# Softmax maxima turned in mid-cycle and loaded right behind their store, in a kernel of attention and a Fourier layer

## The chip, the cores and the metric

One Trainium2 core runs the kernel. The metric is device time in microseconds (us), lower is better. The median of three runs of the kernel before is 1861.64 us (1859.5 to 1863.29).

## The reference

For a sequence of 2048 rows of width 640 it computes gated attention plus a Fourier layer, in float32:

```python
q, k, v = split(x @ wqkv)                     # 32 heads of 20
p = softmax(q @ k.T * 20 ** -0.5)             # per head, 2048 x 2048
a = (p @ v) @ wo
b = Re(DFT_seq(DFT_hidden(x2)))               # as products with given cosine and sine matrices
out = g * a + (1 - g) * b                     # g = sigmoid(sum(x * gate_w)) per row
```

## The kernel before, in words

**Units.** Two heads and half of the queries (1024) are one unit: 32 units, each of 32 steps. There are two passes over the scores of a unit. The maxima pass (`s_mm`, matmul L198, kind `m`) multiplies queries by keys, 128 x 512 scores at a time, and VectorE (DVE) takes the row maximum of each piece (L200). The exponential pass (`score`, matmul L951, kind `e`) multiplies keys by queries into the transposed scores, and ScalarE (ACT) takes the exponential (L953). Each step has two matmuls of each kind, one a head (`h`). The maxima pass runs `LEAD` = 41 steps ahead of the exponential pass.

**What ties the passes.** Queries and keys stand in `qst` and `kst` as 60 rows (three parts of 20). In the exponential pass the matmul has 62 rows: rows 60 and 61 of the queries hold the negative maximum, as a rounded value and a remainder, against ones in the keys. So the first L951 of a unit needs these rows. `max_chain` makes them: four small DVE operations, L228 to L232, of which the last (a transpose into `mtt`) is what "turned" means; then `store` (L235) writes `mtt` to the DRAM tensor `m_scr`, and `rows` (L239) loads two rows for each head from it into the query tile, with two DMAs. Since DRAM lies between, the SP queue waits at L239 until the store has landed.

**The order of work** is written out by hand. A cycle is a string such as the one of phase 1, `ORDERS[1]`:

```python
"ememeFFFFmeFFemFeFmFemFeFeFmeFFmeFFFFmmemmB"
```

`F` are matmuls of the Fourier layer (L637, in phase 0 L380, in phases 2 and 3 L744 for the output product) from split operands `part` and `x` into the banks `yp`. `B` is the burst: 24 matmuls of probabilities by values (L558), and small work, among it `max_chain` of any unit that has ended in the cycle (list `ends`). Phase 0 has 56 cycles of 4 steps, phase 1 (steps 224 to 896) 112 cycles of 6 steps, phases 2 and 3 32 cycles of 4. Since 32 steps are five cycles of six and two steps, the last maximum of a unit in phase 1 is by turns the 4th, the 8th or the 12th of a cycle's twelve maxima: units 10, 13, 16, 19, 22, 25, 28 end at the 4th, units 8, 11, 14, ... 26 at the 8th, units 9, 12, 15, ... 27 at the 12th. All have `max_chain` in the burst.

**Places for scores.** Both passes write to a ring of five PSUM banks (`ps`); a matmul can start when the score matmul five before it has been read, by DVE or by ACT.

**Queues.** `at_step(i, fn)` puts `fn` at the start of step i of the exponential pass (`begin`). It sets only the place in the program: an engine or queue runs its instructions in this order, each when its waits end. Nearly all DMAs go through SP's queue, where a DMA that waits holds up those behind it: loads of 512 KB from the DFT matrices (`raw<-in_cdft`, L512, two in most cycles of phase 1, each into one of three `raw` buffers which GpSimd, POOL, has to have freed), loads of the hidden product (`araw<-a_scr`, L536), partial results (`yt`, L629 and L777), and the sums of the softmax (`r_scr`, L582, whose value DVE's reciprocal makes; `rb`, L586).

Of the kernel before, what the change touches and what calls it, by code (L numbers as in the profile page):

```python
# [72 lines left out]
def f32(ap):  # L73
    return ap.bitcast(F32)
# [3 lines left out]
def mix_kernel(ctx: ExitStack, tc: tile.TileContext, xa, wqk, wb, cdft, wo, out):  # L78
# [50 lines left out]
    def bank():  # L129
        places.rotate(-1)  # L130
        return place_tile(places[-1])
# [41 lines left out]
    def k_stack(n):  # L173
        p = VISITS[n][0]
        return third["k"] if p == 14 else kst[place(p)]

    def q_unit(n):
        p, u = VISITS[n]
        return third["q"] if p == 14 else qst[place(p)][:, u * (S // 2) : (u + 1) * (S // 2)]

    mx, ends = {}, []
    now, later = [-1], {}

    def at_step(i, fn):
        later.setdefault(i, []).append(fn)


    def s_mm(i, h):
        n, s = divmod(i, 32)
        if n >= NU:  # L190
            return lambda: None
        qt, kc = divmod(s, 4)
        q, k = q_unit(n), k_stack(n)
        if n not in mx:
            mx[n] = small.tile([P, 2, 8, 4], F32, name="mx", bufs=2)
        ps = bank()
        b = 64 * h
        pe.matmul(ps, q[b : b + KROWS, qt * P : (qt + 1) * P],  # L198
                  k[b : b + KROWS, kc * 512 : (kc + 1) * 512], start=True, stop=True)
        return lambda: dve.tensor_reduce(mx[n][:, h, qt, kc : kc + 1], ps, axis=AX.X, op=ALU.max)  # L200

    def s_end(i):
        n, s = divmod(i, 32)
        if n < NU and s == 31:
            if now[0] < 0:
                max_chain(n)
            else:
                ends.append(n)
# [14 lines left out]
    def max_chain(n):  # L223
        q = q_unit(n)
        top = mx.pop(n)
        t, tt = small.tile([P, 64], F32, name="mt"), small.tile([P, 32], F32, name="mtt")
        m = t.rearrange("p (x h z c) -> p x z h c", x=2, h=2, z=2)
        dve.tensor_reduce(m[:, 1, 0], top, axis=AX.X, op=ALU.max)  # L228
        dve.tensor_reduce(m[:, 0, 0].bitcast(R), top, axis=AX.X, op=ALU.max, negate=True)
        with nc.allow_low_precision(reason="a remainder, subtracted in float32 and rounded as a part"):  # L230
            dve.tensor_reduce(m[:, 0, 1].bitcast(R), m[:, :, 0].rearrange("p x h c -> p h c x"), axis=AX.X, op=ALU.add, negate=True)
        dve.transpose(tt, t[:, :32])  # L232

        def store():
            sp.dma_start(m_scr[n].rearrange("j b c -> b j c"), tt)  # L235

        def rows():
            for h in range(2):
                sp.dma_start(f32(q[64 * h + KROWS : 64 * h + KROWS + 2, :]),  # L239
                             m_scr[n, 16 * h : 16 * h + 16].rearrange("(z t) b c -> z (t b c)", z=2))  # L240

        if now[0] < 0:
            store()
            rows()
        else:
            at_step(now[0] + 1, store)
            at_step(now[0] + 3, rows)


    pa = pools(name="att", bufs=1)  # L250
# [193 lines left out]
    order = [1, ND + 1, 2, ND + 2, 3, ND + 3, 4, ND + 4]  # L444
# [16 lines left out]
    for n, c in enumerate(order):  # L461
        for t in range(4):
            m = 4 * n + t
# [204 lines left out]
    yo, opre, rows = {}, {}, []  # L668
# [126 lines left out]
    def run_loads(c):  # L795
        while preps["loaded"]:
            preps["combined"].append(preps["loaded"].pop(0))
            preps["combined"][-1][0]()
        n = c // (2 * HT) + 1
        if n < len(PRODUCTS):  # L800
            k = made.get(n, 0)
            made[n] = min(NS, k + 1 + (c % 4 == 3))
            preps["loaded"].extend(load_a(n, s) for s in range(k, made[n]))
# [33 lines left out]
    def phase(c):  # L837
        if c < HID:
            return 0, 0, 4 * c
        if c < edge[-1]:  # L840
            return 1, start, start + 6 * (c - HID)
        i = out_start + 4 * (c - edge[-1])
        return 2 + (i + LEAD >= total), out_start, i
# [38 lines left out]
    def fill(c):  # L882
        nonlocal done
        goal = goals[c].pop(0) if c in goals else 0
        while done < goal:
            next(fills)
            done += 1

    def begin(i):
        now[0] = i  # L890
        n, s = divmod(i, 32)
        for fn in later.pop(i, ()):
            fn()
        if s % 2 == 0:
            flush()
        if s == 0 and n + 1 < NU:
            at_step(i + 6, functools.partial(load_v, n + 1))
        if s == 0:
            load = ()
            if n % 2 == 0 and n < 26:  # L900
                load = load_stack(n // 2 + 1)
            elif n == 25:
                renew(1)
                free = group(1, 1).rearrange("p s z c -> p (s z c)")[:, 4 * HE :]
                third["k"], third["q"] = free[:, :S], free[:, S : S + S // 2]
                pool.memset(f32(third["k"]), 1.0)
                load = itertools.chain(load_k(third["k"], 14), load_q(third["q"], 14, (0, 2)))
            elif n == 26:
                load = load_stack(15)
            elif n == 28:  # L910
                load = load_q(third["q"], 14, (2, 4))
            for j, args in enumerate(load):
                at_step(i + 2 + j, functools.partial(sp.dma_start, *args))
        if i < total:
            pts[n, s // 2, s % 2] = pair_tile()

    def end(i):
        if i % 4 == 2:
            c = i // 4
            if c + HEAD in (NS, 2 * NS):  # L920
                at_step(i + 2, load_wb(3 + (c + HEAD) // NS, pool, pool))
            k = c - HID + NS
            if k in FIRST_A:
                for s in range(FIRST_A[k], FIRST_A[k] + 2):
                    at_step(i + 3, functools.partial(finished, load_a(0, s)))
            if k in (9, 12):
                at_step(i + 4, functools.partial(finished, load_c((k - 9) // 3)))
            if k == 15:
                cfin.append(load_c(2))
# [3 lines left out]
    def score(kind):  # L933
        x = heads[kind]
        heads[kind] += 1
        i, z = divmod(x, 2)
        h = z ^ first[kind][(i - (LEAD if kind == "m" else 0) - 1 - base) % len(first[kind])]
        if kind == "m":
            s_mm(i, h)()
            if z:  # L940
                s_end(i)
            return
        if z == 0 and i <= total:
            begin(i)
        if i < total:
            n, s = divmod(i, 32)
            kt, qc = divmod(s, 2)
            q, k = q_unit(n), k_stack(n)
            b = 64 * h
            pt = bank()  # L950
            pe.matmul(pt, k[b : b + KROWS + 2, kt * P : (kt + 1) * P],  # L951
                      q[b : b + KROWS + 2, qc * 512 : (qc + 1) * 512], start=True, stop=True)
            act.activation(pts[n, kt, qc][:, h], pt, AF.Exp, scale=float(DH) ** -0.5)  # L953
            if z:
                end(i)

    def burst(c):
        k, _, i = phase(c)
        steps = 6 if k == 1 else 4
        run_extras(steps - 2)  # L960
        while ends:
            max_chain(ends.pop(0))
        if k == 1:
            run_casts()
        for kt in range(i // 2, (i + steps) // 2):
            av_step(now[0], kt // NS, kt % NS, kt % NS == 0 and kt > i // 2)
        if c in (HID - NS - 1, HID - 1):
            next_pool()
# [4 lines left out]
    for c in range(len(goals)):  # L973
        k, base, i = phase(c)
        order, *heads_ = ORDERS[k]
        first = dict(zip("em", heads_))
        for x, kind in enumerate(order):
            if kind == "F":
                fill(c)
            elif kind == "B":  # L980
                burst(c)
            else:
                score(kind)
            if k == 1 and x == len(order) // 2:
                run_loads(c - HID)
    assert done == at_goal
# [113 lines left out]
```

## Time and profile before

| | |
|---|---|
| median of 3 runs | 1861.64 us |
| the profiled execution | 1865.62 us, span from first to last instruction 1863.8 us |
| TensorE (PE) busy | 1843.4 us, 99% |
| DVE, ACT, POOL busy | 1379.8, 1356.2, 1002.7 us |
| mean granted TensorE clock | 0.996 |

A busy PE counts matmuls with modelled ends, so 99% doesn't mean that PE is at its peak. It does mean that a time in which PE is idle stands out: in phase 1 the cycles follow each other evenly, and the ones that are longer can be counted one by one. The profile's times are us from the start of the span.

### The profile page before, as it was taken

Reading aid. Unit: us, or ns where it says so; the run is one execution under the profiler, and the core shown is the slowest. Engines: PE = TensorE matmul, PEld = TensorE weight load, DVE = VectorE, ACT = ScalarE, POOL = GpSimd, SP = SyncE. Lnnn points to the kernel's source line nnn. Section 1 sums busy time; section 2 is a strip of 40 time slices with the busy share of each in tenths; the row PEclk is TensorE's granted clock in tenths of the full one; section 3 lists DMA queues with packets and bytes.
Section 4 is the critical chain, followed back from the end, with each engine's and each line's share of the span. In section 5 each row is a group of like instructions: output and inputs, shape, how many; then the busy total and the mean of one; then the engine's idle time right before and its main releaser. Section 6 shows DMA issues by size and latency. Waiting matters only on the chain.

```text
span 1863.8 us, 44701 instructions
## 1 busy us (share of the span) xinstructions
PE 1843.4 (99%) x17574; PEld 1363.1 (73%) x17574; DVE 1379.8 (74%) x2341; ACT 1356.2 (73%) x2645; POOL 1002.7 (54%) x832
## 2 busy tenths in 40 slices
PE   9999999999999999999999999999999999999998
PEld 8988777676767777777677777777767777776666
DVE  3044457887878888888788788888878888888853
ACT  4222257887888888888788788888878877778885
POOL 3335432121136676344578688656668767745544
PEclk9999999999999999999999999999999999999999
DMA  7754341222134683545567576647475856531233
GB/s 229 165 143 152 139 130 56 79 65 69 54 106 135 204 242 126 144 132 177 188 190 245 163 236 211 183 138 197 137 202 192 245 162 189 193 91 55 82 98 109
DMA packets 181202, 282.12 MB, mean 151 GB/s; under 512 B 48139, under 2 KB 115851, under 8 KB 180991
## 3 DMA queue, kind: packets, MB, share of 16 engines
q1 hardware_dynamic: 180031, 277.29, 49.5%
q0 software_dynamic: 960, 1.97, 0.6%
q8 instruction: 138, 2.26, 0.5%
q14 instruction: 73, 0.60, 0.1%
HBM read 215.14 MB, written 64.05 MB: 150 GB/s over the span
## 4 chain that ended last, share of the span: by engine, by line
PE 95%; DMA 2%; POOL 1%; issue 1%; ACT 1%; SPq 0%; DVE 0%; POOLq 0%; ACTq 0%
PE ps L558 24%; PE yp L637 19%; PE ps L951 16%; PE ps L198 14%; PE yp L380 7%; PE ps L120 4%; PE ps L121 4%; PE ps L122 4%; PE yp L744 3%; DMA qst<-m_scr 1%; ACT p L953 1%; POOL part L117 1%; DMA p<-in_xa 0%; DMA a_scr<-raw 0%; DVE mx L200 0%
## 5 line engine op out<-in xcount | busy, mean ns | idle before, releaser
L200 DVE TENSOR_REDUCE mx<-ps 128x1 f32<-128x512 f32 x2048 | 1280.1, 683 | 327.4 <-PE ps L198 274.4
L953 ACT ACTIVATE p<-ps 128x512 f32<-128x512 f32 x2048 | 1054.6, 612 | 289.8 <-PE ps L198 156.0
L951 PE MATMUL ps<-qst,kst 62*128 62x512 f32 x1920 | 726.9, 406 | 10.5 <-DMA qst<-m_scr 9.7
L198 PE MATMUL ps<-kst,qst 60*128 60x512 f32 x1920 | 666.8, 411 | 0.9 <-DVE mx L200 0.9
L637 PE MATMUL yp<-x,part 64*128 64x320 f32 x5376 | 631.3, 307 | 0.0
L637 PEld LDWEIGHTS yp<-x,part 64*128 64x128 f32 x5376 | 602.9, 186 | 5.4
L558 PE MATMUL ps<-p,v 128*21 128x512 f32 (+1 forms) x4096 | 480.7, 597 | 0.0
L117 POOL TENSOR_TENSOR part<-raw,part 128x1024 fp32r<-128x1024 f32 (+1 forms) x128 | 287.6, 2247 | 349.9 <-ACT part L114 344.7
L951 PEld LDWEIGHTS ps<-qst,kst 62*128 62x128 f32 x1920 | 341.8, 185 | 174.8 <-DVE mx L200 86.4
L198 PEld LDWEIGHTS ps<-kst,qst 60*128 60x128 f32 x1920 | 323.7, 185 | 13.4 <-issue 4.2
L558 PEld LDWEIGHTS ps<-p,v 128*21 128x21 f32 (+1 forms) x4096 | 104.1, 101 | 247.2 <-issue 240.0
L380 PE MATMUL yp<-wb,x 64*128 64x320 f32 x1920 | 224.0, 307 | 0.2 <-ACT raw L390 0.2
L380 PEld LDWEIGHTS yp<-wb,x 64*128 64x128 f32 x1920 | 210.0, 186 | 6.6 <-ACT raw L390 0.6
L391 POOL TENSOR_TENSOR raw<-raw 128x320 f32<-128x320 f32 x64 | 55.7, 870 | 263.6 <-ACT raw L390 213.3
L517 POOL TENSOR_TENSOR raw<-raw,raw 128x1024 f32<-128x1024 f32 x77 | 186.4, 2421 | 0.1
L114 ACT ACTIVATE part<-raw 128x1024 fp32r<-128x1024 f32 (+2 forms) x121 | 123.4, 1020 | 2.3 <-DMA raw<-in_wqk 2.2
L744 PE MATMUL yp<-x,part 64*128 64x320 f32 x768 | 102.3, 308 | 0.0
L340 ACT ACTIVATE p<-ps 128x512 f32<-128x512 f32 x40 | 23.8, 597 | 102.6 <-PE ps L122 99.5
L117 POOL TENSOR_TENSOR x<-araw,x 128x320 fp32r<-128x320 f32 x112 | 97.5, 877 | 1.3
L744 PEld LDWEIGHTS yp<-x,part 64*128 64x128 f32 x768 | 92.0, 186 | 1.2
L120 PE MATMUL ps<-x,part 128*128 128x512 f32 x200 | 80.4, 402 | 2.1 <-ACT x L114 1.9
L121 PE MATMUL ps<-x,part 128*128 128x512 f32 x200 | 79.2, 396 | 0.2 <-DVE x L117 0.2
(100 smaller groups left out, 1349.2 us busy)
## 6 DMA issues: line engine op xcount, KB each, us to landing
raw<-in_cdft SPq DMA_DIRECT2D x192, 512.0 KB
araw<-a_scr SPq DMA_DIRECT2D x192, 160.0 KB
qk_scr<-p SPq DMA_DIRECT2D x40, 512.0 KB
kst<-qk_scr SPq DMA_DIRECT2D x84, 160.0 KB
qst<-qk_scr SPq DMA_DIRECT2D x84, 160.0 KB
yt<-y_scr SPq DMA_DIRECT2D x80, 160.0 KB
a_scr<-raw SPq DMA_DIRECT2D x64, 160.0 KB
y_scr<-yt SPq DMA_DIRECT2D x64, 160.0 KB
```

What stands on the lines that cost most here:

```text
L117: e2.tensor_tensor(dst2, src, f32(dst1), op=ALU.subtract)
L120: pe.matmul(ps, st1, mv1, start=first, stop=False)
L121: pe.matmul(ps, st1, mv2, start=False, stop=False)
L198: pe.matmul(ps, q[b : b + KROWS, qt * P : (qt + 1) * P], k[b : b + KROWS, kc * 512 : (kc + 1) * 512], start=True, stop=True)
L200: return lambda: dve.tensor_reduce(mx[n][:, h, qt, kc : kc + 1], ps, axis=AX.X, op=ALU.max)
L380: pe.matmul(yp[h][:, :HE], x[r, xz, d, cs], w[r, wz, d, :HE], start=d == 0 and z == 0, stop=d == ND - 1 and z == 2)
L517: pool.tensor_tensor(raws[0], raws[0], raws[1], op=ALU.add if PRODUCTS[n][0][1][0] > 0 else ALU.subtract)
L558: pe.matmul(t[32 * j : 32 * j + m, :], v[:, r : r + m], pp[qc][:, h, :], start=kt == 0, stop=kt == NS - 1)
L637: pe.matmul(yp[h][:, :HE], c[r, cz, cs], a[r, az], start=s == 0 and z == 0, stop=s == NS - 1 and z == 2)
L744: pe.matmul(yp[h][:, :HE], o[oz][r], wos[d, hf][r, wz], start=d == 0 and z == 0, stop=end)
L951: pe.matmul(pt, k[b : b + KROWS + 2, kt * P : (kt + 1) * P], q[b : b + KROWS + 2, qc * 512 : (qc + 1) * 512], start=True, stop=True)
L953: act.activation(pts[n, kt, qc][:, h], pt, AF.Exp, scale=float(DH) ** -0.5)
```

## The change

Two lines. `rows` is placed one step earlier, so that it follows `store` by one step and not by two. And in phase 1, a unit whose last maximum has come by the eighth maximum of the cycle gets its `max_chain` there, behind the eighth, and not in the burst. That meets the units that end at the 4th and at the 8th maximum, 14 units; those that end at the 12th keep theirs in the burst.

```diff
         else:
             at_step(now[0] + 1, store)
-            at_step(now[0] + 3, rows)
+            at_step(now[0] + 2, rows)
...
             else:
                 score(kind)
+                if k == 1 and kind == "m" and ends and order[: x + 1].count("m") == 8:
+                    max_chain(ends.pop(0))
```

How it moves instructions is seen at three places.

DVE, the chain of unit 13 (ended at the 4th maximum); the first row is the eighth maximum of the cycle. Before:

```order
L200 TENSOR_REDUCE mx<-ps_12992 128x1
L200 TENSOR_REDUCE mx<-ps_13011 128x1
L200 TENSOR_REDUCE mx<-ps_13014 128x1
L200 TENSOR_REDUCE mx<-ps_13020 128x1
L200 TENSOR_REDUCE mx<-ps_13023 128x1
L228 TENSOR_REDUCE mt<-mx 128x2x8
L229 TENSOR_REDUCE mt<-mx 128x2x8
L231 TENSOR_REDUCE mt<-mt 128x2x8
L232 STREAM_TRANSPOSE mtt<-mt 128x32
```

After:

```order
L200 TENSOR_REDUCE mx<-ps_12992 128x1
L228 TENSOR_REDUCE mt<-mx 128x2x8
L229 TENSOR_REDUCE mt<-mx 128x2x8
L231 TENSOR_REDUCE mt<-mt 128x2x8
L232 STREAM_TRANSPOSE mtt<-mt 128x32
L200 TENSOR_REDUCE mx<-ps_13018 128x1
L200 TENSOR_REDUCE mx<-ps_13021 128x1
L200 TENSOR_REDUCE mx<-ps_13027 128x1
L200 TENSOR_REDUCE mx<-ps_13030 128x1
```

The chain has moved ahead of the last four maxima of the cycle.

SP's queue at the store and the rows of unit 13. Before:

```order
L582 DMA r_scr<-lc 128x16
L235 DMA m_scr<-mtt 4x32x32
L512 DMA raw<-in_cdft 128x1024
L512 DMA raw_13069<-in_cdft 128x1024
L629 DMA yt<-y_scr 128x320
L239 DMA qst_89<-m_scr 2x1024 x2
L586 DMA rb<-r_scr 32x512 x4
```

After:

```order
L235 DMA m_scr<-mtt 4x32x32
L582 DMA r_scr<-lc 128x16
L239 DMA qst_89<-m_scr 2x1024 x2
L512 DMA raw<-in_cdft 128x1024
L512 DMA raw_13071<-in_cdft 128x1024
L629 DMA yt<-y_scr 128x320
L586 DMA rb<-r_scr 32x512 x4
```

The rows have moved past two loads of 512 KB and one of 160 KB, and the store past the store of the sums. At unit 15, which ends at the 12th maximum, the rows pass the same three loads, and the store stays where it was.

DVE, the chain of unit 14 (ended at the 8th maximum), where the Fourier layer finishes a tile in the same burst (L657 reads its bank `yp`). Before:

```order
L200 TENSOR_REDUCE mx<-ps_13834 128x1
L657 TENSOR_TENSOR m<-yp_13550,m 128x320
L228 TENSOR_REDUCE mt<-mx 128x2x8
L229 TENSOR_REDUCE mt<-mx 128x2x8
L231 TENSOR_REDUCE mt<-mt 128x2x8
L232 STREAM_TRANSPOSE mtt<-mt 128x32
```

After:

```order
L232 STREAM_TRANSPOSE mtt<-mt 128x32
L200 TENSOR_REDUCE mx<-ps_13829 128x1
L200 TENSOR_REDUCE mx<-ps_13832 128x1
L200 TENSOR_REDUCE mx<-ps_13838 128x1
L200 TENSOR_REDUCE mx<-ps_13841 128x1
L657 TENSOR_TENSOR m<-yp_13550,m 128x320
```

The chain stood behind L657 and now stands ahead of the four maxima that L657 waits behind.

## The prediction

> **What bounds the kernel now.** I read the page first: PE is busy 99% of the span, so only time that PE loses counts. Next, PE's own waits:
>
> ```profile
> PE ps L951 <- DMA qst<-m_scr: 9.7, 4, 3.4
> ...
> PE ps L951 <- ACT p L953: 0.6, 1, 0.6
> ```
>
> Columns: total us, times, longest. The first row is by far the largest: the first exponential matmul of four units waits for its rows. The second is a fifth unit's. Third, the chain that ended last, of which I keep the bursts (start, us, what), because the time from burst to burst is the length of a cycle:
>
> ```profile
> 878.00 2.70 PE ps L558 x24
> 900.72 2.71 PE ps L558 x24
> ...
> 1031.02 2.71 PE ps L558 x24
> 1062.89 2.71 PE ps L558 x24
> ...
> 1193.22 2.70 PE ps L558 x24
> 1203.42 2.70 PE ps L558 x24
> ...
> 1324.38 2.70 PE ps L558 x24
> 1366.78 2.71 PE ps L558 x24
> ...
> 1487.70 2.70 PE ps L558 x24
> 1508.38 2.70 PE ps L558 x24
> ...
> 1648.29 2.70 PE ps L558 x24
> 1657.91 2.70 PE ps L558 x24
> ```
>
> From 1062.89 to 1193.22 lie 14 undisturbed cycles: 130.33 / 14 = 9.309 us each. Against this the pairs above have 2, 3, 1, 4, 2 and 1 cycles, and are longer by 22.72 - 18.62 = 4.10, 31.87 - 27.93 = 3.94, 10.20 - 9.31 = 0.89, 42.40 - 37.24 = 5.16, 20.68 - 18.62 = 2.06 and 9.62 - 9.31 = 0.31 us. The sum is 16.46 us. These are the starts of units 13, 16, 19, 22, 25 and 28, all of the kind that ends at the 4th maximum. That is more than PE's idle time there; the clock has the rest. The timeline of PE shows the idle times in brackets, the windows the granted clock behind four of them (start:end us, busy times, then the clock, the DMA share and GB/s):
>
> ```profile
> 897.47 0.76 PE L951 MATMUL ps<-qst,kst 62*128 62x512 f32 x1 [2.45 <-DMA qst<-m_scr]
> 1354.07 0.47 PE L951 MATMUL ps<-qst,kst 62*128 62x512 f32 x1 [3.35 <-DMA qst<-m_scr]
> ...
> 897.32:900.73 3.41, 3.26 (x22) 2.64 (x26) 0.82 (x2) 1.00 (x2) 0.00 (x0) 0.50 0.89 273
> 1050.91:1054.32 3.41, 3.41 (x21) 1.48 (x21) 2.37 (x4) 2.21 (x4) 0.00 (x0) 0.50 0.90 256
> 1354.70:1358.11 3.41, 3.41 (x22) 1.73 (x23) 2.12 (x4) 2.16 (x4) 0.00 (x0) 0.50 0.92 268
> 1506.50:1509.91 3.41, 3.38 (x34) 1.95 (x38) 1.95 (x4) 2.32 (x4) 1.81 (x1) 1.00 0.17 56
> ```
>
> After the three longest waits PE gets half its clock for 3.41 us, which loses 1.7 us each, 5.1 us together. The wait before 1506.53 has full clock behind it. [...]
>
> **Why the rows come late.** Unit 13 in SP's queue and on DVE:
>
> ```profile
> 882.57 4.00 DVE L200 TENSOR_REDUCE mx<-ps 128x1 f32<-128x512 f32 x6
> 886.88 2.48 DVE L200 TENSOR_REDUCE mx<-ps 128x1 f32<-128x512 f32 x4 [0.31 <-PE ps L198]
> 889.28 0.21 DVE L228 TENSOR_REDUCE mt<-mx 128x16 f32<-128x64 f32 x1
> 889.87 0.21 DVE L232 STREAM_TRANSPOSE mtt<-mt 128x32 f32<-128x32 f32 x1
> ...
> 882.68 0.33 SPq L582 DMA_DIRECT2D r_scr<-lc  x1
> 890.11 0.55 SPq L235 DMA_DIRECT2D m_scr<-mtt  x1
> 890.76 0.89 SPq L512 DMA_DIRECT2D raw<-in_cdft  x2
> ...
> 892.22 0.56 SPq L239 DMA_DIRECT2D qst<-m_scr  x2
> ...
> 892.00:896.00 4.00, 3.03 (x35) 2.71 (x31) 3.58 (x6) 3.54 (x8) 1.49 (x1) 1.00 0.97 333
> ```
>
> The chain ends at 890.08, the rows are issued from 892.22, and the matmul gets them at 897.47, 5.2 us later; meanwhile the 16 DMA engines are 97% busy with the loads issued just ahead. The same distance in unit 28, whose store has two smaller loads behind it, is short:
>
> ```profile
> 1654.01 0.54 SPq L239 DMA_DIRECT2D qst<-m_scr  x2
> 1656.08 0.46 PE L951 MATMUL ps<-qst,kst 62*128 62x512 f32 x1
> ```
>
> There the rows are in place 2.07 us after their first issue at the latest.
>
> **Term 1, the chain behind the eighth maximum.** The eighth maximum of this cycle is the last of the six, which end at 886.57. The chain takes 890.08 - 889.28 = 0.80 us, so `mtt` is there at 887.37 instead of 890.08: 2.7 us earlier. SP has nothing else to wait for in front of it: `r_scr` went out at 882.68, and all that stands ahead of it in the program before.
>
> **Term 2, the rows ahead of the loads.** The store goes out at about 887.4. Between the starts of store and rows lie at least 1.94 us, where nothing stands between them:
>
> ```profile
> 1696.86 0.52 SPq L235 DMA_DIRECT2D m_scr<-mtt  x1
> 1698.80 0.55 SPq L239 DMA_DIRECT2D qst<-m_scr  x2
> ...
> 880.00:890.00 10.00, 10.00 (x106) 6.90 (x98) 8.69 (x19) 7.09 (x14) 7.49 (x5) 1.00 0.02 3
> ```
>
> So the rows go out at 889.4, with the DMA engines at 2% of use (the window). The landing is not shown for this order; its ends are the 2.07 us of unit 28 and the slowest before, unit 22:
>
> ```profile
> 1345.82 0.55 SPq L235 DMA_DIRECT2D m_scr<-mtt  x1
> 1348.40 0.64 SPq L239 DMA_DIRECT2D qst<-m_scr  x2
> ```
>
> From 1348.40 to 1354.07 are 5.67 us. Undisturbed, unit 13's first matmul would come at 897.47 - 2.45 = 895.02. With 2.07 us the rows are there at 891.5, 3.5 us early; with 5.67 us at 895.1, late by 0.05 us. Unit 22 has the longest wait: store at 1345.82 - 2.7 = 1343.1, rows at 1345.1, there at 1347.1 to 1350.7, needed at 1354.07 - 3.35 = 1350.72. I take the short end, as the engines are idle as before unit 28's rows. By either end the six waits go, and with them the half clock: 16.46 us. Either term alone would nearly do. [...]
>
> **Term 3, DVE in mid-cycle.** The chain now delays the last four maxima by 0.80 - 0.31 (idle before them) = 0.5 us, in 14 units. At the worst PE waits for each: 14 x 0.5 = 7.0 us. At the best nothing, for these four are read while PE runs the burst: in unit 13 they would end at about 889.8, and of the ring of five banks the last one's is taken up by the third exponential matmul behind the burst, at 890.5. In the units ending at the 8th maximum (7) L657 also comes later, which frees `yp` for the first L637:
>
> ```profile
> 939.98 0.48 DVE L657 TENSOR_TENSOR m<-yp,m 128x320 f32<-128x320 f32 x1
> ...
> 941.21 0.98 PE L637 MATMUL yp<-x,part 64*128 64x320 f32 x9
> ```
>
> Its end goes from 940.46 to 940.96; the matmul starts at 941.21, its weights a little earlier. That leaves a quarter of a us. I take 0.05 us for each of the 7, 0.4 us in all, close to the cover that these rows show.
>
> **Term 4, SP.** SP now stands idle from the end of the store's issue to the rows (about 1.4 us) where it issued loads before. For units that end at the 4th maximum that falls earlier than the old loads (rows out by 890.0, old loads at 890.76): nothing. For those at the 12th, the loads come about 2 us later. Unit 15:
>
> ```profile
> 988.02 0.94 SPq L512 DMA_DIRECT2D raw<-in_cdft  x2
> ...
> 998.73 2.41 POOL L517 TENSOR_TENSOR raw<-raw,raw 128x1024 f32<-128x1024 f32 x1
> ```
>
> POOL combines these at 998.73, 10.7 us after the issue. With 2 us of delay and 5.67 us for the slowest landing above, 3 us are left: nothing. In phases 0, 2 and 3 only the rows' place moves; no cycle there waits for rows, and stores or loads behind them have a cycle of 6 us as cover: nothing. If that cover were gone, each us of SP's standing would be one of PE's.
>
> **The sum.** -16.46 + 0.4 = -16.1 us. The profiled execution, 1865.62 us with a span of 1863.8, becomes 1849.5 and 1847.7. It is 4 us above the median of the runs, so I subtract from the median: 1861.64 - 16.1 = 1845.5 us.
>
> **Rivals.**
> - *Only the idle time comes back* (0.04): half clock strikes somewhere else, since PE would be idle in shorter pieces. The four waits and the 0.6 give 10.3 us, so 1851.3 us. Against it: the 1.81 us wait had full clock behind it.
> - *DVE becomes the wait* (0.07): the four maxima each hold PE up, 7.0 us, 1861.64 - 16.46 + 7.0 = 1852.2 us. For it: DVE has no idle time between the ninth maximum and L657. Against it: the distances under term 3.
> - *The rows aren't what counts, or the change doesn't bring them forward* (0.05): the L951 would wait equally long for a bank, or SP would reach the store late because a load ahead of it waits for POOL. 1861.6 us. Against it: the releaser is the DMA in four of four, and the same matmul waits in no other cycle.
> - *SP's standing starves POOL* (0.04), the slower one: 21 units of phase 1 at 1.4 us of standing is 29 us, less the 16.5 gained: 1874 us. It decides from the point where the loads come later than the 3 us left in unit 15. Against it: that margin.
>
> **How the numbers follow.** The forecast, all six waits gone, has 0.80. Within 0.2% (3.7 us) a measurement can't tell a change from none. Faster: 0.80 + 0.04 + 0.07 = 0.91; same 0.05; slower 0.04. The range reaches from all 16.46 us with the lowest run of three (2.1 us under the median) at 1843, rounded down to 1842.5, to the first rival at 1851.3: 1842.5 to 1851.5, with 0.84.
>
> **What would show it.** Right: no PE wait on `qst<-m_scr`, the clock at 1.00 through phase 1, cycles of 9.3 us at units 13 to 28, the four operations of the chain ahead of four reductions, rows out before the loads. Term 3 wrong: cycles with a mid-cycle chain longer than 9.31 us. Term 4 wrong: POOL waiting for `raw<-in_cdft`. A remaining half clock would show the first rival.

## The result, and the profile after

The changed kernel takes 1847.86 us (median of 6 runs, 1844.86 to 1849.04) against 1861.76 us of the kernel before (6 runs, 1859.16 to 1863.29): ratio 0.9924, 95% interval 0.9911 to 0.9937. The forecast was 1845.5 us in a range of 1842.5 to 1851.5. The profiled execution went from 1865.62 to 1849.04 us, its span from 1863.8 to 1847.2.

PE's own waits after the change (total us, times, longest):

```profile
PE ps L120 <- ACT x L114: 1.9, 1, 1.9
PE ps L418 <- POOL ident masks.py:199: 1.4, 1, 1.4
PE ps L198 <- DVE mx L200: 0.8, 1, 0.8
PE ps L121 <- DVE x L117: 0.2, 1, 0.2
PE yp L380 <- ACT raw L390: 0.2, 1, 0.2
```

No exponential matmul waits for its rows any more. The first and the last burst of phase 1 on the chain that ended last, first of before, then of after (start, us):

```profile
608.20 2.71 PE ps L558 x24
```

```profile
608.86 2.71 PE ps L558 x24
...
1641.68 2.70 PE ps L558 x24
```

Before, the last burst stands at 1657.91 (shown ahead), so these 111 cycles took 1049.71 us; now they take 1032.82, 9.305 us each and 9.34 at the longest, with a granted clock of 1.00 over the whole stretch. That is 16.89 us less, and 16.6 us is what the span has lost. The runs' median has lost 13.9 us, with an interval of about 11.7 to 16.6. The first burst of phase 0 begins at 257.17 us in the profile of e2 (below) and at 260.42 in that of the changed kernel, so executions differ by some 3 us before any of these cycles: the profile's difference inside phase 1 is the more exact number.

Unit 13 in SP's queue and on DVE, to be read beside the same rows of before:

```profile
883.85 3.29 DVE L200 TENSOR_REDUCE mx<-ps 128x1 f32<-128x512 f32 x5
887.06 0.21 DVE L228 TENSOR_REDUCE mt<-mx 128x16 f32<-128x64 f32 x1
887.86 0.21 DVE L232 STREAM_TRANSPOSE mtt<-mt 128x32 f32<-128x32 f32 x1 [0.24 <-DVE mt L231]
888.00 2.44 DVE L200 TENSOR_REDUCE mx<-ps 128x1 f32<-128x512 f32 x4
...
888.10 0.54 SPq L235 DMA_DIRECT2D m_scr<-mtt  x1
888.70 0.56 SPq L582 DMA_DIRECT2D r_scr<-lc  x1
890.24 0.55 SPq L239 DMA_DIRECT2D qst<-m_scr  x2
890.89 0.83 SPq L512 DMA_DIRECT2D raw<-in_cdft  x2
```

The chain stands ahead of four reductions, and the rows go out ahead of the loads. At the first burst of phase 1 this execution is 0.66 us later than the one of before, which has to be taken off when the two are compared.

### The profile page after: what moved, and what is told of

Its sections match the earlier page's. It is cut to its first block, busy times and chain, and to the rows that moved or that the text cites. A ratio compares the mean times of both kernels' runs of the same rounds, so it can differ in the third digit from the quotient of the medians.

```text
span 1847.2 us, 44690 instructions
## 1 busy us (share of the span) xinstructions
PE 1837.3 (99%) x17574; PEld 1361.3 (74%) x17574; DVE 1378.2 (75%) x2341; ACT 1355.2 (73%) x2645; POOL 1003.0 (54%) x832
## 4 chain that ended last, share of the span: by engine, by line
PE 98%; DMA 1%; POOL 0%; DVE 0%; issue 0%; ACT 0%; SPq 0%; POOLq 0%; ACTq 0%
PE ps L558 25%; PE yp L637 20%; PE ps L951 17%; PE ps L198 14%; PE yp L380 7%; PE ps L120 4%; PE ps L122 4%; PE ps L121 4%; PE yp L744 3%; DMA p<-in_xa 0%; DMA a_scr<-raw 0%; DVE mx L200 0%; PE ps L1036 0%; POOL x L117 0%; POOL raw L391 0%
## 5 line engine op out<-in xcount | busy, mean ns | idle before, releaser
L637 PE MATMUL yp<-x,part 64*128 64x320 f32 x5376 | 627.5, 306 | 0.0
L637 PEld LDWEIGHTS yp<-x,part 64*128 64x128 f32 x5376 | 602.0, 186 | 5.3
```

Of the source, the lines that this page charges most:

```text
L637: pe.matmul(yp[h][:, :HE], c[r, cz, cs], a[r, az], start=s == 0 and z == 0, stop=s == NS - 1 and z == 2)
```

## The experiments

In the profiles the length of phase 1, from its first to its last burst, is compared: 1032.82 us in the changed kernel, 1049.71 in the one before.

**e1, the rows' step alone.** The kernel before with

```diff
-            at_step(now[0] + 3, rows)
+            at_step(now[0] + 2, rows)
```

> The kernel before with one line of the change: rows one step after the store, all chains still in the burst. In SP's queue the rows of units 13 to 28 then stand ahead of the two 512 KB loads. My theory (the place in the queue is what counts): the store of unit 13 goes out at about 890.1, the rows at 892.1, they are there 2.1 us later at 894.2, before the 895.0 at which PE wants them; unit 22 has 0.9 us to spare. All six waits go, phase 1 loses 16 to 17 us, time 1845 to 1849 us. Rival (landing takes its 5 us wherever the rows stand): the waits of units 13, 16, 22 and 25 shrink by less than 0.6 us each, time 1858 to 1861 us.

Measured: 1847.71 us, ratio 0.9927 (0.9912 to 0.9942) to the kernel before; phase 1 is 1033.34 us long. Unit 13:

```profile
889.19 0.54 SPq L235 DMA_DIRECT2D m_scr<-mtt  x1
891.15 0.56 SPq L239 DMA_DIRECT2D qst<-m_scr  x2
891.80 0.83 SPq L512 DMA_DIRECT2D raw<-in_cdft  x2
...
893.94 0.40 PE L951 MATMUL ps<-qst,kst 62*128 62x512 f32 x1
```

The matmul follows the rows' issue by 2.79 us, without waiting. Before, it waited until 5.25 us behind it. So with the chain as late as ever, the place ahead of the loads takes all waits for rows away.

**e2, the turning alone.** The changed kernel with the step back at `+ 3`.

> The changed kernel with rows two steps after the store as before; the chains stay behind the eighth maximum. For the units that end at the 4th maximum the store then falls into the cycle before, and SP's order at store and rows is the same as in the changed kernel. Both theories that were on record expect all six waits gone and 1845 to 1849 us: if so, the step between store and rows brought nothing by itself, and only units that never waited (ending at the 8th or 12th maximum) have it.

Measured: 1845.73 us, ratio 0.9917 (0.9902 to 0.9931); phase 1 is 1033.20 us long, no wait for rows. As expected, the second line also puts the rows ahead of the loads, for the units that waited. At unit 13 the matmul comes 5.3 us behind the rows' issue.

**e3, the turning alone, with the rows behind the loads.** The changed kernel with

```diff
-            at_step(now[0] + 2, rows)
+            at_step(now[0] + 4, rows)
```

> The changed kernel with rows four steps after the store was due to be placed: the chain stays 2.7 us earlier, but the rows stand behind the two 512 KB loads and the yt load again. My theory (queue): those loads wait for POOL until about the same time as before, so the rows go out at most 0.5 us earlier than before (about 892) and land 5 us later: waits of 1.5 to 3.3 us come back at units 13, 16, 22 and 25, phase 1 is 11 to 17 us longer than in the changed kernel, time 1858 to 1862 us. Rival (what counts is that the maxima are turned earlier, term 1 of the prediction alone would nearly do): no waits or under 0.7 us, time 1845 to 1850 us.

Measured: 1847.65 us, ratio 0.9928 (0.9911 to 0.9945); phase 1 is 1033.76 us. My theory's figure was wrong, the rival's right. Unit 13:

```profile
884.93 0.55 SPq L235 DMA_DIRECT2D m_scr<-mtt  x1
885.53 0.46 SPq L582 DMA_DIRECT2D r_scr<-lc  x1
886.09 1.18 SPq L512 DMA_DIRECT2D raw<-in_cdft  x2
887.32 0.42 SPq L629 DMA_DIRECT2D yt<-y_scr  x1
887.84 0.55 SPq L239 DMA_DIRECT2D qst<-m_scr  x2
...
892.70 0.46 PE L951 MATMUL ps<-qst,kst 62*128 62x512 f32 x1 [0.27 <-DMA qst<-m_scr]
```

The loads go out right behind the earlier store. They had not been held by POOL; they had stood behind the store, which waited for the chain, and so the rows come earlier with them. The landing is as slow as before, 4.86 us from issue to matmul, and PE waits 0.27 us for it at this one unit. Phase 1 is 0.9 us longer than in the changed kernel, 0.5 of it in this cycle. So the first line alone takes all waits away (e1), and the earlier turning alone nearly all: it brings the start forward by about 2.7 us, the place ahead of the loads shortens the landing by 2.5 us or more, and the longest wait was 3.4 us.

**e7 and e8, one and two DRAM copies between store and rows,** in phase 1:

```diff
             sp.dma_start(m_scr[n].rearrange("j b c -> b j c"), tt)
+            for i in range(1 if 224 <= now[0] < 896 else 0):       # e8: 2
+                sp.dma_start(m_hop[i][n], src[0][n])
+                src[0] = m_hop[i]
```

and the rows read `src[0][n]`.

> The changed kernel with SP's standing doubled in phase 1: the stored maxima are first copied from DRAM to DRAM by one more DMA, which waits for the store, and the rows wait for the copy. The rows go out about 2 us later (unit 13 at about 892.2). If a landing takes about 2.1 us behind quiet queues they are there at 894.3, before 895.4: no wait, 1847 us, and loads that come 2 us later still cost nothing. If a landing takes 4 us or more, PE waits 0.8 us or more at each of the seven units. If SP's standing costs PE time (the fourth rival of the prediction), phase 1 grows by up to 2 us a unit, 40 us in all, with POOL waiting for raw<-in_cdft.

Measured in one run: 1848.11 us, phase 1 1032.88 us, no wait for rows. At the units that end at the 4th maximum the rows leave 3.9 to 4.3 us behind the store instead of 2.0 to 2.6; at those that end at the 12th, where the loads are the later for it, 3.9 to 6.4 us. Phase 1 is no longer for it. But POOL's combination of the loads waits for them at five places, 5.1 us in all, where it never does in the changed kernel.

> The changed kernel with two DRAM copies between store and rows in phase 1. With one copy the rows went out 3.9 us behind the store's start, with two that is 5.9; the first exponential matmul of the units that end at the 4th maximum comes 7.3 us behind it. If rows ahead of the loads land 2.1 us behind their issue, PE waits 0.3 to 0.7 us at each of the seven units, too short for half clock, 2 to 5 us in all; if they land within 1.4 us, not at all; with 5 us, 3.6 us each and half clock. Of SP's standing: the loads are 4 us later than in the changed kernel where a unit ends at the 12th maximum, so POOL waits for raw<-in_cdft, some 2 to 4 us a time in 7 units (5.1 us in all with one copy); whether PE feels it tells where the fourth rival begins.

Measured in one run: 1854.78 us, phase 1 1039.18 us, 6.4 more than the changed kernel. PE, and SP's rows at unit 13:

```profile
894.06 0.56 SPq L245 DMA_DIRECT2D qst<-m_hop  x2
...
746.28 0.46 PE L957 MATMUL ps<-qst,kst 62*128 62x512 f32 x1 [0.47 <-DMA qst<-m_hop]
896.14 0.47 PE L957 MATMUL ps<-qst,kst 62*128 62x512 f32 x1 [0.71 <-DMA qst<-m_hop]
...
1182.86 0.50 PE L199 MATMUL ps<-kst,qst 60*128 60x512 f32 x1 [0.58 <-ACT p L959]
```

Now all seven units wait 0.27 to 0.71 us (PE's list puts two of these waits down to ACT, but their matmuls come just as long behind the rows), and so the landing is seen: 896.14 - 894.06 = 2.08 us from the first row's issue, 1.96 to 2.08 over the seven. Their seven cycles are 0.5 to 1.0 us longer, 5.3 in all. The third PE row belongs to no unit's start. It is the fourth rival: POOL's and ACT's rows there show how a late load gets to PE,

```profile
1177.42 2.37 POOL L523 TENSOR_TENSOR raw<-raw,raw 128x1024 f32<-128x1024 f32 x1 [1.87 <-DMA raw<-in_cdft]
1179.83 1.06 ACT L115 ACTIVATE part<-raw 128x1024 fp32r<-128x1024 f32 x1 [1.11 <-POOL raw L523]
```

POOL's combination waits for the load, ACT's split for POOL, and behind the split ACT has the exponentials that PE's banks wait for. POOL waits for these loads 12.1 us in all with two copies, 5.1 us with one, and only the 12.1 reach PE, about 1 us at one place in 112 cycles (the cycle from 1177.88 takes 10.32 us).

**e5 and e6, more DVE work in mid-cycle.** The changed kernel with L228, L229 and L231 done twice (e5) or four times (e6) behind the eighth maximum; same values.

> The changed kernel with the first three operations of the chain (L228, L229, L231) done twice where it stands behind the eighth maximum: 0.6 us more of DVE in mid-cycle, 14 times. Theory (the cover of term 3 is nearly used up: from the end of the cycle's last maximum to the matmul that takes its bank at least 0.5 us are left in the changed kernel, from L657 to the first L637 about 0.1 to 0.3): units ending at the 8th maximum lose 0.3 to 0.5 us each, those at the 4th 0 to 0.2, phase 1 grows by 2 to 5 us, PE with small waits on DVE at L637. Rival (DVE in mid-cycle is free): phase 1 within 0.5 us of the changed kernel's.

> The same with the three operations done four times: 1.8 us more of DVE, 14 times. Theory: what goes beyond the cover falls on PE, 1.2 to 1.6 us a unit, phase 1 grows by 16 to 22 us and the kernel is about as slow as the one before, 1862 to 1869 us. Rival (free): as the changed kernel.

Measured in one run each: 1849.9 and 1866.7 us; phase 1 is 1035.39 and 1051.40 us, 2.6 and 18.6 us longer than in the changed kernel. Bursts of e5 around the chain of unit 14, then of e6 around those of units 14 and 13:

```profile
933.56 2.70 PE ps L559 x24
943.22 2.70 PE ps L559 x24
952.51 2.70 PE ps L559 x24
```

```profile
929.58 2.70 PE ps L559 x24
949.73 2.70 PE ps L559 x24
...
881.96 2.70 PE ps L559 x24
901.65 2.70 PE ps L559 x24
```

With 0.6 us more, the cycle behind the chain of a unit that ends at the 8th maximum is 9.66 us instead of 9.31, and the units that end at the 4th lose nothing. With 1.8 us more, the two cycles of the first kind take 20.15 us (1.54 over), of the second 19.69 (1.07 over). So the changed kernel has about 0.25 us of cover left for the first kind and 0.7 for the second; what exceeds it falls on PE one to one. PE's list of waits shows nothing of it in e5: only the lengths of the cycles do. What the first kind waits for is seen in e5 behind the burst at 933.56 (its L658 and L638 are L657 and L637 here):

```profile
936.57 0.48 DVE L658 TENSOR_TENSOR m<-yp,m 128x320 f32<-128x320 f32 x1
937.04 1.07 PE L638 MATMUL yp<-x,part 64*128 64x320 f32 x11
```

The first Fourier matmul starts as L658 ends, 0.85 us behind the burst's first exponential matmul (936.19); in the cycle before it is 0.58 us. That is 0.27 of the 0.35 us. The second kind has no L657 in its burst.

**e9, later rows in the kernel before** (`+ 6` for `+ 3`), to see what a wait costs.

> The kernel before with rows five steps after the store instead of two: at units 13 to 28 they stand behind the loads and behind the four rb loads. Waits grow by 1.5 to 2.5 us at each of the seven units that end at the 4th maximum. Theory of the sum (idle time plus half of 3.4 us of half clock once a wait exceeds about 2 us): phase 1 is longer than an undisturbed one by PE's idle time plus 1.7 us for each of the 5 to 7 waits of over 2 us, some 20 + 10 = 30 us, time 1872 to 1882 us. Rival (what comes beyond the idle time is a restart cost of every wait): the excess over idle is the same for short and long waits.

Measured in one run: 1869.89 us; phase 1 is 1056.45 us, 23.6 more than in the changed kernel, below what I expected. PE waits for rows 16.8 us, 8 times: at the seven units that end at the 4th maximum and at unit 8. The PE row of unit 13, then windows of 3.41 us that end where half clock starts or, by the spacing measured in the kernel before (last section), could start, and what comes behind unit 13:

```profile
897.58 0.46 PE L951 MATMUL ps<-qst,kst 62*128 62x512 f32 x1 [2.64 <-DMA qst<-m_scr]
...
893.35:896.76 3.41, 1.58 (x18) 1.29 (x16) 2.32 (x4) 2.10 (x5) 0.08 (x1) 1.00 0.91 312
1046.95:1050.36 3.41, 1.05 (x14) 1.08 (x16) 0.66 (x2) 0.88 (x2) 0.00 (x0) 1.00 0.68 205
1350.73:1354.14 3.41, 0.30 (x4) 0.01 (x1) 1.15 (x2) 0.82 (x2) 0.00 (x0) 1.00 0.71 215
1507.74:1511.15 3.41, 1.66 (x18) 1.44 (x18) 0.25 (x1) 0.61 (x2) 0.26 (x1) 1.00 0.21 64
...
896.76:900.17 3.41, 2.59 (x26) 1.70 (x30) 1.18 (x2) 1.55 (x4) 0.00 (x0) 1.00 0.77 234
1050.36:1053.77 3.41, 3.41 (x21) 1.15 (x21) 2.88 (x5) 1.92 (x4) 0.50 (x1) 0.50 1.00 337
```

Unit 13 waits 2.64 us and keeps full clock, though 2.45 us brought half clock before. Only units 16 and 22 are followed by half clock, 3.41 and 6.83 us of it, which lose 5.1 us. 16.8 + 5.1 leaves 1.7 us for the 8 waits, 0.2 us each. My expectation, half clock behind each wait of over 2 us, is wrong; so is the rival's, one cost for all waits.

**e10, the rows from ACT's queue** in the kernel before, at the same place:

```diff
-                sp.dma_start(f32(q[64 * h + KROWS : 64 * h + KROWS + 2, :]),
+                (sp if now[0] < 0 else act).dma_start(f32(q[64 * h + KROWS : 64 * h + KROWS + 2, :]),
```

> The kernel before with the rows, from phase 0 on, issued by ACT's queue instead of SP's, at the same place in the program: they go out at about the same time as before (unit 13 some 2 to 2.5 us behind the store's start), while the two 512 KB loads that SP issued just ahead are under way, but they don't stand behind them in SP's queue. Theory Q (what held the rows was the queue's order): they land 2 to 2.5 us behind their issue, nearly all waits of units 13 to 28 go, phase 1 is within 3 us of the changed kernel's, 1846 to 1852 us. Theory E (what held them is the DMA engines being busy with the loads, whichever queue issued these): they land 4 to 5.5 us behind their issue as before, and phase 1 stays 12 to 18 us longer, 1858 to 1864 us.

Measured in one run: 1885.89 us, phase 1 1061.28 us. Unit 13:

```profile
902.09 0.89 SPq L512 DMA_DIRECT2D raw<-in_cdft  x2
903.41 0.54 ACTq L239 DMA_DIRECT2D qst<-m_scr  x2
...
908.03 0.47 PE L951 MATMUL ps<-qst,kst 62*128 62x512 f32 x1 [1.52 <-DMA qst<-m_scr]
...
PE ps L198 <- ACT p L953: 10.0, 10, 3.9
PE ps L951 <- DMA qst<-m_scr: 8.9, 6, 2.1
```

From another queue, with the loads under way (the DMA engines 97% busy from 904 to 906 us), the rows still need 4.62 us here, and 3.9 to 5.2 at the six units that wait for them (last row). ACT's queue isn't slow by itself. The trace also records when the semaphore of each of the two row DMAs rises for the last time: at unit 1, where the DMA engines are 18% busy, that is 1.55 and 1.53 us behind the issue; at unit 18, where they are 93% busy, 4.16 and 4.45. In the changed kernel, ahead of the loads, it is 1.5 to 1.7 us at units 8 to 27. So theory E holds for the landing, as far as these runs show it: the rows are slow where the DMA engines are busy with loads that were issued earlier, 4.91 and 4.82 us at unit 13 of the kernel before, from SP's queue, and 4.16 and 4.45 at unit 18 here, from ACT's.

The time of 1885.89 us fits neither theory: phase 1 is 28.5 us longer than in the changed kernel, not 12 to 18. Besides 8.9 us for rows, PE waits 10.0 us for exponentials (the row above it), since ACT takes none while it stands at the rows. At units 12 and 21 ACT is idle there for 2.2 and 4.1 us, as the second row's DMA goes out 2.3 and 4.2 us behind the first. What held it is not shown; it wasn't the store, which the first row had waited for. The rest of the 28.5 us stays open.

## Why the prediction was right, step by step

- *The waits go, 16.46 us.* Phase 1 has lost 16.89 us. The five waits of PE's list are gone (unit 28 had none, only a cycle 0.31 us longer), and with them the three stretches of half clock: the clock is 1.00 through phase 1, so the first rival is out. Counting the cycles' lengths and not PE's idle time was what made the size right: by idle time alone it would have been 10.3 us. Of the 0.43 us beyond 16.46, 0.27 are a longer cycle from 1564.27 that I hadn't counted. It belongs to no unit's start, and e1, e2 and e3 have one like it. Its cause is open, and that it is missing here is not shown to be the change's doing.
- *Term 1, 2.7 us earlier.* The store went out at 888.10; less the 0.66 us of the later start that is 887.44, against 887.4. Right, and e3 shows it to be enough by itself but for 0.27 us at one unit.
- *Term 2, the landing.* I put its ends at 2.07 and 5.67 us and took the short one. e8 measures 1.96 to 2.08 us ahead of the loads, e3 4.86 behind them. The cause that I gave, loads issued just ahead, is shown by e1; e10, with 4.62 us from ACT's queue, speaks for the busy engines and against the order in SP's queue.
- *Term 3, 0.4 us.* Measured: nothing, since the changed kernel's cycles are 9.305 us on average, the undisturbed ones of before 9.309. The quarter of a us of cover behind L657 was right: e5 uses it up.
- *Term 4, nothing.* Right for PE, but the 3 us that I thought were left before POOL waits were too many. In e7 the rows of unit 9 go out 2.1 us later behind their store than in the changed kernel, and POOL already waits 0.68 us for the loads, until 7.3 us behind their issue and not 5.67: about 1.4 us were left. PE felt none of the 5.1 us of e7, so there is more cover between POOL and PE, which I hadn't counted; in e8 it is used up at one place.
- *Half clock, 1.7 us each.* Right for these three within about 0.2 us: what their cycles have lost beyond PE's wait is 4.10 - 2.45 = 1.65, 3.94 - 2.11 = 1.83 and 5.16 - 3.35 = 1.81 us (unit 25, with full clock behind it, 2.06 - 1.81 = 0.25). But what I built on it for e9 was too simple: that a wait of over about 2 us is enough for half clock (2.11 us at unit 16 was followed by it before, 2.64 at unit 13 of e9 was not). It didn't enter the sum, as all waits went.
- *The total.* 16.1 us were forecast, 16.6 lost in the profiled span, 13.9 in the medians. That the medians lost less is within their interval; nothing in the profile of phase 1 stands for it.

None of the versions beats the changed kernel clearly: e1, e2 and the changed kernel have overlapping intervals, and the same phase 1 within about 0.5 us. What the changed kernel has over e1 is margin: at unit 13 the matmul comes 5.2 us behind the rows' issue instead of 2.8 (at unit 28 of e1 only 2.1), where a quiet landing takes 2.0. Over e2 it has none, as e2 has 5.3 us there: the margin is the second line's.

## What to carry to other kernels

A small transfer that an engine waits for should be issued ahead of large loads, not behind them: from issue to matmul it took 2.0 us ahead of them (e8) and 4.9 behind (e3). Going to another queue didn't help, since with the loads already under way it took 4.6 us there too (e10). A wait's price is read from the length of the cycle around it, not from the engine's idle time, as the clock may fall behind it: here to 0.50 for 3.41 us, behind three of the waits. And before putting work in the middle of a full cycle, count the cover from that place to the next use of each buffer: here 0.25 us were left at the tightest, and all beyond was paid one to one (e6: 1.54 us of the 1.8 added).

## What the runs showed of the hardware that I had not expected

Half clock came in windows of 3.41 us that don't follow the waits. In the kernel before, the trace's record of the clock has three of them in phase 1, each 3.413 us long, from 897.32, 1050.91 and 1354.70. Their starts are 153.59 and 303.79 us apart, which is 45.0 and 89.0 times 3.413. The first begins 0.15 us before the wait of unit 13 ends, the second and third 0.77 and 0.63 us behind the ends of those of units 16 and 22. The wait of unit 16:

```profile
1050.14 0.47 PE L951 MATMUL ps<-qst,kst 62*128 62x512 f32 x1 [2.11 <-DMA qst<-m_scr]
```

The windows just ahead of the three falls, and the one around the wait of unit 25, in the kernel before (second number: PE busy):

```profile
893.91:897.32 3.41, 1.12 (x14) 0.82 (x10) 1.85 (x3) 1.63 (x4) 0.00 (x0) 1.00 0.88 305
1047.50:1050.91 3.41, 1.30 (x17) 1.05 (x16) 1.29 (x2) 1.30 (x4) 0.00 (x0) 1.00 0.72 228
1351.29:1354.70 3.41, 0.64 (x8) 0.67 (x10) 0.26 (x1) 0.13 (x1) 0.00 (x0) 1.00 0.54 173
1504.88:1508.30 3.42, 1.77 (x18) 1.45 (x18) 1.02 (x3) 1.06 (x3) 0.36 (x1) 1.00 0.52 155
```

With e9's rows: PE busy 0.30, 0.64, 1.05, 1.12 and 1.30 us of 3.41 were followed by half clock, 1.58, 1.66 and 1.77 us were not. So of two waits of about the same length one was followed by half clock (2.45 us, before) and the other was not (2.64 us, e9); that it depends on where the wait falls in the window is my estimate from these rows. But PE's busy time doesn't decide by itself, as e10 shows in phase 0:

```profile
541.06:544.47 3.41, 1.89 (x17) 0.79 (x18) 1.73 (x3) 2.13 (x5) 0.00 (x0) 1.00 0.71 227
544.48:547.89 3.41, 3.41 (x18) 1.15 (x12) 0.40 (x2) 0.94 (x4) 2.50 (x4) 0.50 0.15 52
564.96:568.37 3.41, 2.03 (x17) 0.64 (x9) 1.40 (x3) 0.98 (x3) 0.14 (x1) 1.00 0.75 130
```

There 1.89 us were followed by half clock (second row), and so were 2.03, 59% of a window. What is counted in a window stays open.
